# Attention and two expert blocks on one core: other start offsets for the matmul operands, and unpadded score products for two pairs of heads

## The chip, the cores and the metric

The kernel runs on one core of one Trainium2 chip. Its engines appear in the profile as PE (TensorE, the matrix engine; PEld is its loading of weights), DVE (VectorE), ACT (ScalarE), POOL (GpSimd) and SP (SyncE, which only issues transfers here). The metric is the device time of one execution in microseconds; less is better.

## What is computed

The reference, cut to what matters:

```python
def _attn_ref(q, k, v):                      # q, k, v: (2, 12, 448, 64)
    scores = scale * np.matmul(q, k.transpose(0, 1, 3, 2))
    mask = np.triu(np.ones((seq, seq), dtype=bool), k=1)
    scores = np.where(mask, -1000000000.0, scores)
    scores = scores - np.max(scores, axis=-1, keepdims=True)
    attn = np.exp(scores)
    attn = attn / (np.sum(attn, axis=-1, keepdims=True) + 1e-09)
    return np.matmul(attn, v).astype(np.float32)

def _moe_ref(x, w_in, w_out, alpha):         # x: (896, 768), w_in: (768, 2048), w_out: (2048, 768)
    h = x @ w_in
    g = np.maximum(h, 0.0) + alpha * np.minimum(h, 0.0)
    return (g @ w_out).astype(np.float32)

def _moe2_ref(x, w_in, w_out):
    h = x @ w_in
    g = np.where(h >= 1, h, np.where(h <= -1, 0.0, (h + 1) ** 2 / 4.0))
    return (g @ w_out).astype(np.float32)
```

The causal attention of 2 batches with 12 heads gives x (896 tokens by 768), which goes through two expert blocks of two matrix products each.

## The kernel before

Everything is in float32 and laid out with the features on the partitions. There are 12 pairs of heads and two batches, so six pairs belong to each batch; a pair fills 128 partitions (two heads of 64 features), and its result is one tile of x. So x has 6 tiles for each batch, `x_t[b, m]`, and the hidden layer g has 16, `g_t[b, f]`. Such a tile is 128 partitions by 2 parts by 448 columns.

The two parts are how the kernel gets precise products. A float32 value is split into a high part that fits the reduced type `float32r` and the rest; a product of two split values is made of three matmuls: high by high, high by rest, rest by high. The function `products` (line 255) does this for the layers: for each slice of 128 input features it runs six matmuls of 448 columns, three for each batch. The weights come as 64-bit floating point numbers, which five DVE and ACT operations (`split_ops`, lines 124 to 148) turn into a float32 value and split into `w_split`, one chunk at a time into three buffers in turn. A chunk is 6 slices of 128 by 128 in layers 1 and 3 and 4 slices in layers 2 and 4; a slice is loaded as the stationary operand, and a tile of x or g streams past it.

The attention of a pair has four steps i of 112 queries each, with 112, 224, 336 and 448 keys (`W`). In `scores`, the step i = 0 is a plain float32 matmul on the loaded data (line 351), and the others are split products (line 357), of which step 1 is padded from 224 to 256 columns. The two heads of a pair lie in different halves of the array's rows, and their matmuls run side by side. `split_qk` (lines 337 and 338) splits q and k of the next pair: ACT makes the high part, POOL the rest; of q, the first 112 columns, which only step 0 uses, are not split. Then follow the exponential (`expo`, ACT), the scaling with the inverse sum (`norm`, DVE and POOL), the transposes (`transp`, PE line 394), the products with v (`attnv`, PE line 413) and the splitting of the result into a tile of x (`evac`).

The order of all work is written out by hand: a loop over t = 0, 1, 2, ... runs, in each turn, the scores of step t, the exponential of step t - 1, the transposes of step t - 3 and the v products seven to nine steps later, and each engine takes its instructions in the order in which the code issues them. Pairs 3 and 4 are the turns t = 12 to 19. At the end of this loop the first products of layer 1 are mixed in (`early_tiles`). Then `run_layer` runs the four layers one after the other; in each turn PE runs the products of one output tile, while DVE, ACT and POOL split the chunk of weights that comes three turns later and work on the output tile of the turn before (the activation and its split in layers 1 and 3, `split_g`; the split of x, or the output, in layers 2 and 4). The last output tile of layer 4 is worked one batch after the other.

All tiles are whole rows of their buffers: x and g tiles of 3584 bytes a partition with their second part at byte 1792, split weights of 6144 bytes with their second part at byte 3072.

Of the kernel before, what the change touches and what calls it, by code (L numbers as in the profile page):

```python
# [9 lines left out]
F32R = mybir.dt.float32r  # L10
# [12 lines left out]
def attention_moe_moe_kernel(ctx: ExitStack, tc: tile.TileContext, qk, v, w1, w2, w3, w4, alpha, out):  # L23
# [8 lines left out]
    nc = tc.nc  # L32
    NP, _, _, S = qk.shape
    NB = 2
    CP, NQ, _, D = v.shape[1:]
# [4 lines left out]
    NF, _, KD, _ = w1.shape  # L40
    NM, NC2, _, KC, _ = w2.shape
# [3 lines left out]

    NSQ = 1
    NWARM = 9

    const = ctx.enter_context(tc.tile_pool(name="const", bufs=1))
    xpool = ctx.enter_context(tc.tile_pool(name="x", bufs=1))  # L50
    wp = ctx.enter_context(tc.tile_pool(name="wp", bufs=2))

    x_t, g_t = {}, {}

    def f32(t):
        return t.bitcast(F32)
# [6 lines left out]
    def warm_up():  # L63

        z = const.tile([128, 512], F32R, tag="zero", name="zero")
        nc.vector.memset(f32(z), 0.0)
        for _ in range(NWARM):
            ps = ps_o.tile([128, 512], F32, tag="o", name="warm_ps")
# [12 lines left out]
    class Weights:  # L81
# [29 lines left out]
        def split_ops(self):  # L111

            if self.n_split == len(self.chunks):
                return []
            n_split = self.n_split
            self.n_split += 1
            (raw, n), w = self.raw.pop(n_split), self.w.pop(n_split)
            words = raw[:, :2 * n].rearrange("p (n two) -> p n two", two=2)
            lo, hi = words[:, :, 0], words[:, :, 1]
            s = self.split[n_split] = wp.tile([128, 2, KD * 128], F32R, tag="w_split", name="w_split", bufs=3)  # L120

            def clamp():

                nc.vector.tensor_scalar(  # L124
                    out=f32(w), in0=f32(w), scalar1=HI_MIN, scalar2=HI_MAX, op0=ALU.max, op1=ALU.min
                )

            def low_bits():

                nc.vector.tensor_scalar(  # L130
                    out=w, in0=w, scalar1=5, scalar2=2, op0=ALU.logical_shift_left, op1=ALU.logical_shift_right
                )

            def high_bits():

                nc.vector.scalar_tensor_tensor(  # L136
                    out=w, in0=hi, scalar=0xC0000000, in1=w, op0=ALU.bitwise_and, op1=ALU.bitwise_or
                )

            def last_bits():  # L140

                nc.vector.scalar_tensor_tensor(  # L142
                    out=w, in0=lo, scalar=29, in1=w, op0=ALU.logical_shift_right, op1=ALU.bitwise_or
                )
                nc.scalar.copy(s[:, 0, :n], f32(w))  # L145

            def rest():
                nc.vector.tensor_sub(s[:, 1, :n], f32(w), f32(s[:, 0, :n]))  # L148

            return [clamp, low_bits, high_bits, last_bits, rest]  # L150

        def prime(self):
# [13 lines left out]
            return self.split.pop(self.n_used - 1)  # L166


    def split_g(g, b, f):
        t = g_t[b, f] = gpool.tile([128, 2, S], F32R, tag=f"g{b}_{f}", name=f"g{b}_{f}", bufs=1)  # L170
        nc.scalar.copy(t[:, 0, :], g)  # L171
        nc.gpsimd.tensor_sub(t[:, 1, :], g, f32(t[:, 0, :]))  # L172

    def act_prelu(ps, f, b):
        t = ep.tile([128, S], F32, tag="act_t", name="act_t")
        g = ep.tile([128, S], F32, tag="act_g", name="act_g")

        def negative():
            nc.vector.tensor_scalar(
                out=t, in0=ps[:, :S], scalar1=0.0, scalar2=alpha_sb[:, f:f + 1], op0=ALU.min, op1=ALU.mult  # L180
            )

        def total():
            nc.vector.scalar_tensor_tensor(out=g, in0=ps[:, :S], scalar=0.0, in1=t, op0=ALU.max, op1=ALU.add)  # L184
            split_g(g, b, f)

        return [negative, total]

    def act_quad(ps, f, b):

        t = ep.tile([128, S], F32, tag="act_t", name="act_t")
        g = ep.tile([128, S], F32, tag="act_g", name="act_g")

        def square():
            nc.vector.tensor_scalar(out=t, in0=ps[:, :S], scalar1=-1.0, scalar2=1.0, op0=ALU.max, op1=ALU.min)  # L195
            nc.scalar.activation(out=t, in_=t, func=AF.Square, bias=half[:, 0:1], scale=0.5)  # L196

        def total():
            nc.vector.tensor_tensor(out=g, in0=ps[:, :S], in1=t, op=ALU.max)
            split_g(g, b, f)  # L200

        return [square, total]

    def evac_x(ps, m, b):
        t = x_t[b, m] = xpool.tile([128, 2, S], F32R, tag=f"x{b}_{m}", name=f"x{b}_{m}", bufs=1)

        def high():
            nc.scalar.copy(t[:, 0, :], ps[:, :S])

        def low():  # L210
            nc.vector.tensor_sub(t[:, 1, :], ps[:, :S], f32(t[:, 0, :]))  # L211

        return [high, low]
# [36 lines left out]
    def products(ps, ws, src, k, kk, first, last):  # L250

        for part in range(2):
            for b in ps:
                for xp in range(2 - part):
                    nc.tensor.matmul(  # L255
                        ps[b][:, :S],
                        lhsT=ws[:, part, k * 128:(k + 1) * 128],
                        rhs=src[b, kk][:, xp, :],
                        start=first and part == 0 and xp == 0,
                        stop=last and part == 1,  # L260
                    )

    def early_tiles(batches):

        for f, bs in enumerate(batches):
            ws = wts.next()
            ps = {b: new_tile() for b in bs}
            early[f] = ws, ps
            for k in range(KD - 1):
                products(ps, ws, x_t, k, k, k == 0, False)  # L270
                yield

    def run_layer(layer, late):
# [3 lines left out]
        else:  # L277
            mt, nch, kc, src = NM, NC2, KC, g_t
        evac = {1: act_prelu, 2: evac_x, 3: act_quad, 4: evac_out}[layer]
        for m in range(mt):  # L280
            ps = {}
# [25 lines left out]
    class Attention:  # L307
# [23 lines left out]
        def split_qk(self, p, a, high=nc.scalar.copy, low=nc.gpsimd):  # L331
            t = self.raw[p]
            if a == 0:
                self.spl[p] = self.ap.tile([2 * D, 2, 2, S], F32R, tag="qk_spl", name="qk_spl", bufs=2)
            s = self.spl[p]
            n0 = NSQ * CP if a == 0 else 0
            high(s[:, a, 0, n0:], t[:, a, n0:])
            low.tensor_sub(s[:, a, 1, n0:], t[:, a, n0:], f32(s[:, a, 0, n0:]))

        def scores(self, p, i):  # L340
            if i == 0:
                self.pexp[p] = self.ap.tile([CP, 2, TRI], F32, tag="pexp", name="pexp", bufs=3)
                self.st[p] = self.ap.tile([CP, NQ, 3, 2], F32, tag="stat", name="stat", bufs=4)
            s, t = self.spl[p], self.raw[p]
            w = W[i]
            n = max(w, 256)
            ps = [self.ps_s.tile([128, 512], F32, tag="s", name="s_ps")[:CP] for _ in range(2)]
            if i < NSQ:
                for j in range(2):
                    r = slice(j * D, (j + 1) * D)  # L350
                    nc.tensor.matmul(  # L351
                        ps[j][:, :w], lhsT=t[r, 0, i * CP:(i + 1) * CP], rhs=t[r, 1, :w], start=True, stop=True
                    )
            for x, (a, b) in enumerate(self.PARTS if i >= NSQ else ()):
                for j in range(2):
                    r = slice(j * D, (j + 1) * D)
                    nc.tensor.matmul(  # L357
                        ps[j][:, :n], lhsT=s[r, 0, a, i * CP:(i + 1) * CP], rhs=s[r, 1, b, :n],
                        start=x == 0, stop=x == 2,
                    )  # L360

            for j in range(2):
                nc.vector.tensor_tensor_reduce(  # L363
                    out=self.pexp[p][:, j, OFF[i]:OFF[i] + w], in0=ps[j][:, :w], in1=mask[:, S - w:],
                    scale=-SCALE, scalar=3.0e38, op0=ALU.add, op1=ALU.min,
                    accum_out=self.st[p][:, i, 0, j:j + 1],
                )
# [50 lines left out]
        def evac(self, p):  # L418
            b, m = divmod(p, NP // NB)
            interleave(evac_x(self.o.pop(p), m, b), [])  # L420

    with tc.manual_schedule():
# [6 lines left out]
        with ExitStack() as pa:  # L429
# [21 lines left out]
            for t in range(NT + LX - 2):  # L451
                p, r = divmod(t, NQ)
# [31 lines left out]
        gpool = ctx.enter_context(tc.tile_pool(name="g", bufs=1))  # L484
# [51 lines left out]
```

## Time and profile before

| | |
|---|---|
| Runs of the kernel, us | 584.26, 586.44, 595.68; median 586.44 |
| Span of the profiled execution, first to last instruction, us | 591.80 |
| Busy time PE, DVE, ACT, POOL, us | 583.1, 442.3, 255.6, 161.6 |
| Granted TensorE clock, mean | 0.999 of full speed |

The runs are without the profiler; the profiled execution is one more, of which only the span is recorded, and its span is the time that its rows add up to. Matmuls are pipelined and the profile models their ends, so that a matmul's own duration (370 ns) is longer than the distance to the next one, and a busy PE isn't PE at its peak: the distance from start to start is what counts.

### The profile page before, as it was taken

How to read it: one execution, taken by the hardware profiler on the slowest of the kernel's cores; microseconds unless marked ns; L12 is line 12 of the kernel's file. 1: busy time of each engine (PE TensorE's matmuls, PEld its weight loads, DVE VectorE, ACT ScalarE, POOL GpSimd, SP SyncE). 2: the span in 40 equal slices, each digit the busy share in tenths (PEclk: the TensorE clock that was granted, in tenths of full speed). 3: DMA queues.
4: the chain of work that ended last, by engine and by line, in shares of the span. 5: the costliest groups of instructions: out<-in, count | busy, mean ns of one | idle time of the engine just before them, and what ended most of it. 6: DMA issues, size and time to landing. Idle time of an engine off the chain costs nothing.

```text
span 591.8 us, 8421 instructions
## 1 busy us (share of the span) xinstructions
PE 583.1 (99%) x3009; PEld 491.8 (83%) x3009; DVE 442.3 (75%) x894; ACT 255.6 (43%) x543; POOL 161.6 (27%) x190
## 2 busy tenths in 40 slices
PE   8999999999999999999999999999999999999997
PEld 3655555789999999999999999999999999999995
DVE  4899998488898898766657668888888867555740
ACT  3889888223333333333223325555555422222220
POOL 3777787223333343000000002333334300000000
PEclk9999999999999999999999999999999999999999
DMA  6533301113333222343324333333322244444420
GB/s 187 201 95 88 131 24 55 54 54 107 108 112 108 109 94 76 107 138 87 99 105 129 120 107 117 108 103 107 107 104 82 67 133 137 136 116 133 138 66 31
DMA packets 18569, 61.88 MB, mean 105 GB/s; under 512 B 2208, under 2 KB 5536, under 8 KB 18528
## 3 DMA queue, kind: packets, MB, share of 16 engines
q1 hardware_dynamic: 16656, 59.75, 32.3%
q10 hardware_dynamic: 1872, 1.61, 0.8%
q8 instruction: 23, 0.38, 0.2%
q14 instruction: 18, 0.15, 0.1%
HBM read 58.60 MB, written 2.75 MB: 104 GB/s over the span
## 4 chain that ended last, share of the span: by engine, by line
PE 95%; DVE 3%; ACT 1%; issue 0%; ACTq 0%; DVEq 0%
PE ps L255 81%; PE o_ps L413 5%; PE t_ps L394 4%; PE s_ps L357 4%; PE warm_ps L69 1%; DVE pexp L363 1%; PE s_ps L351 1%; DVE stat L380 0%; DVE pt L405 0%; DVE w_f L142 0%; DVE x L211 0%; ACT w_split L145 0%; ACT pexp L373 0%; DVE stat L381 0%; DVE pt L402 0%
## 5 line engine op out<-in xcount | busy, mean ns | idle before, releaser
L255 PE MATMUL ps<-x,w_split 128*128 128x448 f32 x1152 | 240.2, 369 | 0.2 <-DVE x L211 0.2
L255 PE MATMUL ps<-g,w_split 128*128 128x448 f32 x1152 | 238.6, 368 | 0.9 <-DVE o_sb L221 0.9
L255 PEld LDWEIGHTS ps<-x,w_split 128*128 128x128 f32 x1152 | 215.7, 188 | 24.4 <-issue 1.7
L255 PEld LDWEIGHTS ps<-g,w_split 128*128 128x128 f32 x1152 | 216.2, 188 | 23.0 <-DVE o_sb L221 1.3
L172 POOL TENSOR_TENSOR g<-act_g,g 128x448 fp32r<-128x448 f32 x64 | 85.6, 1337 | 281.4 <-ACT g L171 281.3
L145 ACT CAST w_split<-w_f 128x512 fp32r<-128x512 f32 (+1 forms) x80 | 56.6, 707 | 130.9 <-DVE w_f L142 90.9
L148 DVE TENSOR_TENSOR w_split<-w_f,w_split 128x512 fp32r<-128x512 f32 (+1 forms) x80 | 66.0, 825 | 53.6 <-ACT w_split L145 53.3
L171 ACT CAST g<-act_g 128x448 fp32r<-128x448 f32 x64 | 36.1, 564 | 79.2 <-DVE act_g L184 69.2
L136 DVE SCALAR_TENSOR_TENSOR w_f<-w_raw,w_f 128x512 uint32<-128x512 uint32 (+1 forms) x80 | 63.4, 793 | 1.4
L142 DVE SCALAR_TENSOR_TENSOR w_f<-w_raw,w_f 128x512 uint32<-128x512 uint32 (+1 forms) x80 | 63.4, 793 | 1.4
L124 DVE TENSOR_SCALAR w_f<-w_f 128x512 f32<-128x512 f32 (+1 forms) x80 | 58.1, 727 | 8.1 <-ACT w_f L108 7.9
L108 ACT ACTIVATE w_f<-w_raw 128x512 f32<-128x512 f32 (+1 forms) x80 | 61.3, 766 | 0.1
L384 POOL TENSOR_SCALAR pexp<-pexp,stat 112x112 f32<-112x112 f32 (+3 forms) x96 | 52.9, 564 | 24.4 <-DVE stat L381 19.3
L373 ACT ACTIVATE pexp<-pexp,stat 112x112 f32<-112x112 f32 (+3 forms) x96 | 49.9, 523 | 4.4 <-DVE stat L363 3.9
L363 DVE CUSTOM_DVE_ANT_0 pexp<-s_ps,mask 112x112 f32<-112x112 f32 (+3 forms) x96 | 39.1, 445 | 7.8 <-PE s_ps L351 4.6
L130 DVE TENSOR_SCALAR w_f<-w_f 128x512 uint32<-128x512 uint32 (+1 forms) x80 | 38.0, 475 | 1.4
L196 ACT ACTIVATE act_t<-act_t,half 128x448 f32<-128x448 f32 x32 | 21.5, 671 | 39.5 <-DVE act_t L195 39.5
L413 PE MATMUL o_ps<-pt,v_raw 112*64 112x448 f32 (+3 forms) x192 | 36.8, 418 | 0.0
L394 PE MATMUL t_ps<-ident,pexp 112*112 112x112 f32 x240 | 34.5, 276 | 0.0
L394 PEld LDWEIGHTS t_ps<-ident,pexp 112*112 112x112 f32 x240 | 23.9, 138 | 10.5 <-issue 5.3
L357 PE MATMUL s_ps<-qk_spl 64*112 64x256 f32 (+2 forms) x216 | 30.3, 374 | 2.2 <-DVE stat L363 2.2
L221 DVE COPY o_sb<-ps 128x224 f32<-128x224 f32 x12 | 4.7, 392 | 32.3 <-ACT o_sb L221 32.3
(38 smaller groups left out, 286.0 us busy)
## 6 DMA issues: line engine op xcount, KB each, us to landing
w_raw<-w SPq DMA_DIRECT2D x32, 768.0 KB, 4.3
w_raw<-w SPq DMA_DIRECT2D x48, 512.0 KB, 3.6
qk_raw<-qk SPq DMA_DIRECT2D x11, 448.0 KB, 3.7
v_raw<-v SPq DMA_DIRECT2D x12, 224.0 KB, 3.2
out<-o_sb SPq DMA_DIRECT2D x12, 112.0 KB, 1.7
out<-o_sb ACTq DMA_DIRECT2D x12, 112.0 KB, 1.7
qk_raw<-qk ACTq DMA_DIRECT2D x1, 224.0 KB, 3.5
qk_raw<-qk SPq DMA_DIRECT2D x1, 224.0 KB, 3.3
```

The lines of the kernel that those rows point to most:

```text
L108: nc.scalar.activation(out=f32(w), in_=f32(hi), func=AF.Abs)
L124: nc.vector.tensor_scalar(out=f32(w), in0=f32(w), scalar1=HI_MIN, scalar2=HI_MAX, op0=ALU.max, op1=ALU.min)
L136: nc.vector.scalar_tensor_tensor(out=w, in0=hi, scalar=0xC0000000, in1=w, op0=ALU.bitwise_and, op1=ALU.bitwise_or)
L142: nc.vector.scalar_tensor_tensor(out=w, in0=lo, scalar=29, in1=w, op0=ALU.logical_shift_right, op1=ALU.bitwise_or)
L145: nc.scalar.copy(s[:, 0, :n], f32(w))
L148: nc.vector.tensor_sub(s[:, 1, :n], f32(w), f32(s[:, 0, :n]))
L172: nc.gpsimd.tensor_sub(t[:, 1, :], g, f32(t[:, 0, :]))
L255: nc.tensor.matmul(ps[b][:, :S], lhsT=ws[:, part, k * 128:(k + 1) * 128], rhs=src[b, kk][:, xp, :], start=first and part == 0 and xp == 0, ...
L357: nc.tensor.matmul(ps[j][:, :n], lhsT=s[r, 0, a, i * CP:(i + 1) * CP], rhs=s[r, 1, b, :n], start=x == 0, stop=x == 2,)
L384: nc.gpsimd.tensor_scalar(out=e, in0=e, scalar1=st[:, 2, j:j + 1], scalar2=1.0, op0=ALU.mult, op1=ALU.mult)
L394: nc.tensor.transpose(ps[:, j, c, :], self.pexp[p][:, j, o:o + CP], ident)
L413: nc.tensor.matmul(ps[j * D:(j + 1) * D, c * CP:S], lhsT=vraw[:, c, j, :], rhs=pt[:, j, c, c * CP:S], start=c == 0, stop=c == NQ - 1,)
```

## The change

Two parts. First, the tiles of x and g become 24 words longer, and a tile's content starts at an offset that depends on its number (0, 8, 24, 4, 2 or 16 words of 4 bytes, taken in turn by m for x and f for g); the buffers of the split weights become 48 words longer, and their two parts start at offsets that depend on the chunk's number. Second, for the pairs 3 and 4 (`BARE`) step 0 of the scores runs as three split products of 112 columns instead of one plain float32 product, step 1 runs on 224 columns without the padding to 256, and so the whole of q is split for these pairs.

```diff
+    BARE = (3, 4)
+    PLACE = (0, 8, 24, 4, 2, 16)
+    WPLACE = ((0, 0), (8, 4), (24, 2))
...
-            s = self.split[n_split] = wp.tile([128, 2, KD * 128], F32R, tag="w_split", name="w_split", bufs=3)
+            t = wp.tile([128, 2 * (KD * 128 + max(PLACE))], F32R, tag="w_split", name="w_split", bufs=3)
+            s = self.split[n_split] = [
+                t[:, o + part * (KD * 128 + max(PLACE)):][:, :KD * 128]
+                for part, o in enumerate(WPLACE[n_split % len(WPLACE)])
+            ]
...
-                nc.scalar.copy(s[:, 0, :n], f32(w))
+                nc.scalar.copy(s[0][:, :n], f32(w))
...
-                nc.vector.tensor_sub(s[:, 1, :n], f32(w), f32(s[:, 0, :n]))
+                nc.vector.tensor_sub(s[1][:, :n], f32(w), f32(s[0][:, :n]))
...
+    def placed(pool, name, i):
+        o = PLACE[i % len(PLACE)]
+        t = pool.tile([128, 2 * S + max(PLACE)], F32R, tag=name, name=name, bufs=1)
+        return t[:, o:o + 2 * S].rearrange("p (x s) -> p x s", x=2)
+
     def split_g(g, b, f):
-        t = g_t[b, f] = gpool.tile([128, 2, S], F32R, tag=f"g{b}_{f}", name=f"g{b}_{f}", bufs=1)
+        t = g_t[b, f] = placed(gpool, f"g{b}_{f}", f)
...
     def evac_x(ps, m, b):
-        t = x_t[b, m] = xpool.tile([128, 2, S], F32R, tag=f"x{b}_{m}", name=f"x{b}_{m}", bufs=1)
+        t = x_t[b, m] = placed(xpool, f"x{b}_{m}", m)
...
-                        lhsT=ws[:, part, k * 128:(k + 1) * 128],
+                        lhsT=ws[part][:, k * 128:(k + 1) * 128],
...
-            n0 = NSQ * CP if a == 0 else 0
+            n0 = NSQ * CP if a == 0 and p not in BARE else 0
...
-            n = max(w, 256)
+            n = w if p in BARE else max(w, 256)
...
-            if i < NSQ:
+            plain = i < NSQ and p not in BARE
+            if plain:
...
-            for x, (a, b) in enumerate(self.PARTS if i >= NSQ else ()):
+            for x, (a, b) in enumerate(() if plain else self.PARTS):
```

## Rows read from the trace of the kernel before

**Rows 1.** The chain of waits: shares of the span by engine, then by line.

```profile
PE 95%; DVE 3%; ACT 1%; issue 0%; ACTq 0%; DVEq 0%
PE ps L255 81%; PE o_ps L413 5%; PE t_ps L394 4%; PE s_ps L357 4%; PE warm_ps L69 1%; DVE pexp L363 1%; PE s_ps L351 1%; DVE stat L380 0%; DVE pt L405 0%; DVE w_f L142 0%; DVE x L211 0%; ACT w_split L145 0%; ACT pexp L373 0%; DVE stat L381 0%; DVE pt L402 0%
```

**Rows 2.** Busy time by stretch: pairs 3 and 4, then the four layers.

```profile
core 0: us, PE busy (x) PEld busy (x) DVE busy (x) ACT busy (x) POOL busy (x), PEclk, DMA share, GB/s
30.90:46.20 15.30, 15.30 (x117) 9.00 (x116) 14.06 (x57) 13.37 (x45) 11.70 (x20) 1.00 0.30 92
...
121.00:238.00 117.00, 117.00 (x568) 106.27 (x567) 105.07 (x148) 41.33 (x64) 42.71 (x32) 1.00 0.29 97
240.00:358.00 118.00, 118.00 (x572) 107.19 (x571) 76.79 (x131) 35.73 (x59) 0.00 (x0) 1.00 0.38 118
360.00:477.00 117.00, 117.00 (x568) 106.28 (x567) 101.23 (x142) 61.61 (x96) 42.85 (x32) 1.00 0.31 97
479.00:584.00 105.00, 105.00 (x510) 95.38 (x509) 58.72 (x108) 26.80 (x49) 0.00 (x0) 1.00 0.38 114
```

**Rows 3.** Groups by line: the layers' products (busy us, mean ns, idle before).

```profile
L255 PE MATMUL ps<-x,w_split 128*128 128x448 f32 x1152 | 240.2, 369 | 0.2 <-DVE x L211 0.2
L255 PE MATMUL ps<-g,w_split 128*128 128x448 f32 x1152 | 238.6, 368 | 0.9 <-DVE o_sb L221 0.9
```

**Rows 4.** Timeline of PE in four windows: start, us, what, count; line 255.

```profile
104.90 2.74 PE L255 MATMUL ps<-x,w_split 128*128 128x448 f32 x12
...
108.86 2.70 PE L255 MATMUL ps<-x,w_split 128*128 128x448 f32 x12
...
112.10 2.07 PE L255 MATMUL ps<-x,w_split 128*128 128x448 f32 x9
...
115.00 1.50 PE L255 MATMUL ps<-x,w_split 128*128 128x448 f32 x6
...
117.15 1.50 PE L255 MATMUL ps<-x,w_split 128*128 128x448 f32 x6
...
119.30 1.18 PE L255 MATMUL ps<-x,w_split 128*128 128x448 f32 x3
...
239.81 105.56 PE L255 MATMUL ps<-g,w_split 128*128 128x448 f32 x510
...
559.73 24.96 PE L255 MATMUL ps<-g,w_split 128*128 128x448 f32 x120
...
585.59 0.67 PE L255 MATMUL ps<-g,w_split 128*128 128x448 f32 x2 [0.90 <-DVE o_sb L221]
...
585.59 2.70 PE L255 MATMUL ps<-g,w_split 128*128 128x448 f32 x12 [0.90 <-DVE o_sb L221]
```

**Rows 5.** Timeline of PE in pair 4; x4 and x6 of one start come from two windows.

```profile
38.55 0.45 PE L351 MATMUL s_ps<-qk_raw 64*112 64x112 f32 x4
38.94 0.59 PE L394 MATMUL t_ps<-ident,pexp 112*112 112x112 f32 x4
...
40.18 0.49 PE L357 MATMUL s_ps<-qk_spl 64*112 64x256 f32 x4
...
40.18 0.61 PE L357 MATMUL s_ps<-qk_spl 64*112 64x256 f32 x6
40.72 0.79 PE L394 MATMUL t_ps<-ident,pexp 112*112 112x112 f32 x6
...
42.80 0.98 PE L394 MATMUL t_ps<-ident,pexp 112*112 112x112 f32 x8
...
43.71 0.66 PE L357 MATMUL s_ps<-qk_spl 64*112 64x448 f32 x4
...
43.71 0.86 PE L357 MATMUL s_ps<-qk_spl 64*112 64x448 f32 x6
```

**Rows 6.** Weight loads of the plain score step: in the timeline, and over all (min/median/max, ns).

```profile
38.55 0.27 PEld L351 LDWEIGHTS s_ps<-qk_raw 64*112 64x112 f32 x4 [0.70 <-issue]
...
L351 PEld LDWEIGHTS s_ps<-qk_raw x48: 169/172/308, 9.0 to 96.2; 64*112 64x112 f32 x48
```

**Rows 7.** Groups by line and form: the splitting of q (336) and k (448).

```profile
L338 POOL TENSOR_TENSOR qk_spl<-qk_raw,qk_spl 128x448 fp32r<-128x448 f32 x11 | 12.6, 1148 | 0.0
...
L338 POOL TENSOR_TENSOR qk_spl<-qk_raw,qk_spl 128x336 fp32r<-128x336 f32 x11 | 9.9, 898 | 6.2 <-ACT qk_spl L337 6.2
...
L337 ACT CAST qk_spl<-qk_raw 128x448 fp32r<-128x448 f32 x11 | 6.2, 566 | 0.0
...
L337 ACT CAST qk_spl<-qk_raw 128x336 fp32r<-128x336 f32 x11 | 5.0, 458 | 5.2 <-DMA qk_raw<-qk 5.2
```

**Rows 8.** Timeline of POOL ahead of the pair that begins at 38.55 us.

```profile
33.75 0.90 POOL L338 TENSOR_TENSOR qk_spl<-qk_raw,qk_spl 128x336 fp32r<-128x336 f32 x1
35.04 0.69 POOL L384 TENSOR_SCALAR pexp<-pexp,stat 112x112 f32<-112x112 f32 x2 [0.40 <-DVE stat L381]
35.70 1.15 POOL L338 TENSOR_TENSOR qk_spl<-qk_raw,qk_spl 128x448 fp32r<-128x448 f32 x1
```

## The prediction

> **What bounds the kernel now.** I read the chain of waits first, then the stretches, then single runs of matmuls. The chain gives TensorE (PE) 95% of the span, and the products of the two expert blocks, line 255, 81% alone [rows 1]. The four layers fill the windows from 121 to 584 us with PE busy all of the time; VectorE (DVE) comes next, 105.07 of 117 us in the first layer and 101.23 in the third, far less in the others [rows 2]. So between 121 and 584 us the time is the number of products times their spacing, and DVE is not late until PE's layer time shrinks by a tenth. Line 255 has 2 x 1152 products [rows 3].
>
> The spacing is the thing to see. From 239.81 us on 510 products take 105.56 us; less the last one's own 0.37 us, that is 509 gaps of 0.2067 us. The 120 products from 559.73 us give (24.96 - 0.37) / 119 = 0.2066. But the last 12, which start anew at 585.59 us, lie closer: two take 0.67 us and twelve 2.70, so ten more cost 2.03, 0.203 each [rows 3, 4]. The 12 at 108.86 us take the same 2.70 us [rows 4]. So one and the same instruction has **two spacings**, 206.7 and about 203 ns; the wider one, once taken, holds over hundreds of products. Of the 2304, 48 stand ahead of 120.66 us and 12 in the last run [rows 4]; the 2,244 between are the ground on which the offsets can win or lose.
>
> Where do these operands lie? One (tile, part) of x or g is 448 words, 1792 bytes, and a 128-column slice of a split weight 512 bytes. Both are multiples of 256. So in the kernel before the starts of all streams of x and g differ by multiples of 256 bytes, those of all weight slices likewise, and the 206.7 ns holds for every k, part, batch and buffer. That excludes an effect of displacements of 256 bytes and more. Nothing in the trace tries smaller ones, and these are what the change brings (8 to 96 bytes within a tile, and 96 more bytes of length per x or g tile).
>
> In the attention stage, 30.9 to 46.2 us (the pairs 3 and 4), PE is busy 15.30 of 15.30 us, DVE 14.06, ACT 13.37, POOL 11.70 [rows 2]: what PE gains or loses there goes to the end nearly one for one, until DVE, 1.24 us behind in two pairs, takes over.
>
> **Part 1: offsets of x, g and the split weights.** No instruction is added, removed or moved; every tile gets longer by at most 192 bytes and every write keeps its shape. The cost is 2,244 times a change of the spacing. Bounds: the wider spacing is the most that the trace shows in a run without a wait, and 203 ns the least for this shape. One hint for whether starts matter: the score products are of the same kind (split operands), and their weight slices begin at multiples of 448 bytes, so at 192, 128 and 64 bytes within 256. At 448 columns their third round costs 0.86 - 0.66 = 0.20 us, at 256 columns 0.61 - 0.49 = 0.12 [rows 5]: 0.45 and 0.47 ns per column, against 0.45 at the closer spacing of line 255 (203 / 448). Other weight starts, the same rate. It looks like a property of the stream, and the wider spacing like the way in which products settle against each other in time. I take **0**; the low end is that all products go to the closer spacing, 2,244 x (206.7 - 203) ns = **-8.3 us**. The high end is a loss of the same size, the only step between spacings that the trace has: six start offsets, of which one is 0, so at 5/6 of the products 2,244 x 5/6 x 3.7 ns = **+6.9 us**.
>
> The Trainium skill (TensorE: Matmul & The Clock Gate, Part 2, step 1) says that TensorE has two independent SBUF read ports, one for the streamed operand and one for the weight load, and that loading the next weights takes no bandwidth from the running matmul. By that rule the placing of x against the weights can't matter and the term is 0; that the spacing takes two values with the same operands, 206.7 and 203 ns [rows 4], shows at least that something beyond the columns enters. The skill (SBUF — State Buffer, Door 1) also states 16-byte lines with a penalty at each crossing; a start 8 bytes into a line makes 113 lines of 112, an estimate of 1/112 of 206.7 ns, 1.8 ns, at the tiles that have that offset (one x tile in six, two g tiles in sixteen: 336 products), 0.6 us. No run here shows it.
>
> The writers: ACT, DVE and POOL write the shifted tiles with the same shapes. Their cover is DVE's 12 us of slack in layer 1 and 16 us in layer 3, and 41 to 46 us in the others [rows 2]; gone only if DVE got 11% slower. Cost 0.
>
> **Part 2: the first two score steps of pairs 3 and 4.** In step 0 a head's plain float32 product (two instructions of 112 columns) becomes three split products of 112 columns. Both heads run side by side, so it is two rounds becoming three. In step 1 three rounds shrink from 256 to 224 columns. Nothing in the trace streams split operands under 256 columns, so I bound it.
> Low end: the stream goes on as it does above 256 columns, and a round lasts as long as the longer of its stream and its weight load. Step 1: a round falls from 0.12 us by 32 x 0.45 ns, three rounds -0.04 us. Step 0: the four weight loads take 0.27 us, of which one's own 0.17 is the tail, so a round of loading is 0.10 us [rows 6]; three such rounds stand for two of about 0.09 to 0.10 (the eight transposes of 112 columns take 0.39 us more than the first four, 0.10 each [rows 5]), the last with 0.05 us less to stream: +0.05 us. Sum 0.01 us a pair.
> High end: under 256 columns a split product costs as much as a plain one. A plain product of 112 columns takes two instructions of some 0.095 us (by the 0.09 to 0.10 above), 0.19; step 0: two more of them, +0.38 us. Step 1: 224 columns cost 0.38 instead of 0.12, three times, +0.78. Sum 1.16 us a pair, **+2.3 us** for both.
> I take the low end, **+0.0**, by the nearest row, the 256-column rounds: the same instruction on the same operands, 32 columns away. Below nothing there is little room: the whole of step 1 is 40.72 - 40.18 = 0.54 us [rows 5].
>
> The q half is now split over 448 instead of 336 columns for these pairs: ACT 0.57 for 0.46 us, POOL 1.15 for 0.90 [rows 7]. On POOL the split of q ends 0.40 us before the next scaling can start, which waits for DVE [rows 8], so 0.25 us are covered; without that cover the k half and the next transposes behind it on POOL would come 0.25 us later. ACT has 1.93 us idle in the two pairs [rows 2]. Step 0 now waits for the split of both halves instead of the raw load; the k half of the pair that begins at 38.55 us is done at 35.70 + 1.15 = 36.85 us, 1.7 us ahead [rows 5, 8]. Cost 0.
>
> **The sum.** 0 + 0.0 + 0 on the profiled execution: its span of 591.80 us stays at about 591.8. The three runs are 584.26, 586.44 and 595.68, so the profiled execution lies between the second and the third. That spread, 11.4 us, is not much more than the 8.3 us between the two spacings over 2,244 products: the runs may differ in how much of each holds the wider spacing. So the run with the median may already lie close, and I carry the difference of 0 to the median: **586.5 us**.
>
> **The rivals.**
> 1. *The shifted starts break the wide spacing.* For it: the wide spacing is one exact value held by 500 products, as two streams in step would give; each k brings another offset and would knock them out of step. Against: the score products above. Gain up to 8.3 us on a run that is wide throughout, less on one that is not: 578 to 584 us, 579 as one number. Chance 0.20.
> 2. *The excess over the clock is a conflict of addresses, and the offsets remove it.* PE's granted clock is 1.00, the 2.4 GHz level [rows 2]; one cycle per column is 186.7 ns for 448 columns, and the plain 112-column instructions come within 2 or 3 ns of their 93.3 (two cycles a column). Without conflicts the spacing would be near 189, 17 ns less, 2,244 x 17 ns = 38 us: 548 us. DVE would still not bind (layer 1: 117 x 189/206.7 = 107 us, DVE 105.07). Against: the score products show the same excess at other weight starts, and it grows with the columns, as the 0.12 and 0.20 us show. Chance 0.06. The isolated matmul of the TensorE page (Back-to-back issue gap) is N/2.4 + 2.5 ns, 189.2 at 448 columns, the same result; the trace has 206.7 and 203.
> 3. *Slower: a start inside a fetched piece of the memory costs each shifted stream one more piece.* It strikes at 5/6 of the products and is never hidden, since PE has no other work. At 3.7 ns it gives 6.9 us, with the high end of part 2 9.2 us: 593 to 596 us. It decides against rival 1 as soon as it exceeds 3.7 ns at each shifted product, and passes 2% (11.7 us) from 6.3 ns. Against: nothing in the trace shows a start that costs. Chance 0.16, of which 0.07 beyond 2%.
> The case that is left is the forecast itself, in which part 1 does not do what offsets could be meant to do, since the products settle against each other whatever their starts: 586.5 us, chance 0.58.
>
> **How the numbers follow.** Two per cent, 11.7 us, is about what a measurement of this kernel can tell from no change. Faster by more (under 574.7): rival 2 and a tail of rival 1, 0.09. Slower by more (over 598.2): 0.07 of rival 3 and 0.01 for part 2 on top of a wide-spaced median, 0.08. Within: 0.83. The range reaches over rival 1 and over rival 3 up to 2%, and takes in a median that lies with the slower of the runs shown: 577 to 597 us.
>
> **What would show it.** If part 1 is right, long runs of line 255 keep 0.2067 us a product, in all four layers. If rival 1 holds, the spacing is mixed, near 0.203; if rival 2, near 0.19; if rival 3, it exceeds 0.207 at the shifted tiles. Part 2 is seen in the score groups of pairs 3 and 4: six products of 112 columns in about 0.5 us and six of 224 in about 0.57 by the low end, 0.83 and 1.4 by the high end, beside 0.45 and 0.61 for pairs that are not changed. The forecast goes wrong if starts within 256 bytes matter to the stream, and little else can move it far.

## The result, and the profile after

The changed kernel took 588.95, 590.07, 593.88 and 593.94 us, median 591.98; the kernel before, with one run more, 584.26, 584.91, 586.44 and 595.68, median 585.67. The ratio is 1.011, 95% interval 1.008 to 1.015: a small loss, inside the forecast range (577 to 597 us) and within 2%, but not the difference of 0 that was forecast.

These times don't scatter around one value. In all timings together the kernel before shows two levels, one around 585 us and one around 594 (a few executions near 599), with little between; 41 of its 82 executions lay above 590 us. In the three series below the granted clock was 0.999 to 1.000 at either level, so it isn't the clock. The share of the upper level was 3 of 24 in the first of them, 21 of 25 in the second and 16 of 29 in the third, and each ran on another chip. A ratio to this kernel therefore depends on how many executions of either level it meets, and below each kernel is set beside the level that it is compared with.

The profiled execution of the changed kernel has a span of 587.2 us, the one of the kernel before had 591.80: in these two executions the changed kernel is the shorter one. The chain by line is still that of [rows 1]: the layers' products, now line 271, 80%.

```profile
PE 95%; DVE 3%; ACT 1%; issue 0%; ACTq 0%; DVEq 0%
PE ps L271 80%; PE o_ps L430 5%; PE t_ps L411 4%; PE s_ps L374 4%; PE warm_ps L76 1%; DVE pexp L380 1%; PE s_ps L368 1%; DVE stat L397 0%; DVE pt L422 0%; DVE w_f L153 0%; DVE x L227 0%; ACT w_split L156 0%; ACT pexp L390 0%; DVE stat L398 0%; DVE pt L419 0%
```

The stretches of [rows 2], here layers 1 and 2 of the kernel after: PE has no gap in layer 2, DVE still has its slack, and more products fit into the same 118 us (580 instead of 572).

```profile
core 0: us, PE busy (x) PEld busy (x) DVE busy (x) ACT busy (x) POOL busy (x), PEclk, DMA share, GB/s
...
121.00:238.00 117.00, 116.80 (x572) 107.17 (x571) 105.72 (x149) 41.64 (x65) 42.11 (x32) 1.00 0.29 97
240.00:358.00 118.00, 118.00 (x580) 108.69 (x579) 78.41 (x134) 36.47 (x61) 0.00 (x0) 1.00 0.38 118
```

The timeline of PE merges products that follow each other without a gap, and a whole layer (96 turns of six) can stand in one row. That makes it the best view for the spacing: (duration - 0.37) / 575. First the kernel before, a window that was not shown with [rows 4], then the kernel after.

```profile
229.88 119.20 PE L255 MATMUL ps<-g,w_split 128*128 128x448 f32 x576
348.93 119.20 PE L255 MATMUL ps<-x,w_split 128*128 128x448 f32 x576
```

```profile
229.75 117.68 PE L271 MATMUL ps<-g,w_split 128*128 128x448 f32 x576
347.26 117.67 PE L271 MATMUL ps<-x,w_split 128*128 128x448 f32 x576
```

That is 206.7 ns before and **204.0 ns** after. From single starts to the next, the trace of before holds 206 or 207 ns through layers 2 and 3; the one after holds everything from 195 to 215 ns, with a mean of 204.0 (the timeline's rows give means; these single distances are taken from the starts of the matmuls in the traces, here and below).

The score steps of pairs 3 and 4, to be read beside [rows 5]: six products of 112 columns in 0.50 us, six of 224 in 0.58 and 0.56, where four plain ones took 0.45 and six of 256 columns 0.61.

```profile
31.93 0.50 PE L374 MATMUL s_ps<-qk_spl 64*112 64x112 f32 x6
...
33.61 0.58 PE L374 MATMUL s_ps<-qk_spl 64*112 64x224 f32 x6
...
38.25 1.65 PE L430 MATMUL o_ps<-pt,v_raw 112*64 112x448 f32 x4
39.83 0.50 PE L374 MATMUL s_ps<-qk_spl 64*112 64x112 f32 x6
...
41.50 0.56 PE L374 MATMUL s_ps<-qk_spl 64*112 64x224 f32 x6
```

### The profile page after: what moved, and what is told of

It reads as the page before. It is cut to its first block, busy times and chain, and to the rows that moved or that the text cites. A ratio compares the mean times of both kernels' runs of the same rounds, so it can differ in the third digit from the quotient of the medians.

```text
span 587.2 us, 8431 instructions
## 1 busy us (share of the span) xinstructions
PE 578.4 (99%) x3013; PEld 493.1 (84%) x3013; DVE 441.5 (75%) x894; ACT 256.3 (44%) x543; POOL 161.0 (27%) x190
## 4 chain that ended last, share of the span: by engine, by line
PE 95%; DVE 3%; ACT 1%; issue 0%; ACTq 0%; DVEq 0%
PE ps L271 80%; PE o_ps L430 5%; PE t_ps L411 4%; PE s_ps L374 4%; PE warm_ps L76 1%; DVE pexp L380 1%; PE s_ps L368 1%; DVE stat L397 0%; DVE pt L422 0%; DVE w_f L153 0%; DVE x L227 0%; ACT w_split L156 0%; ACT pexp L390 0%; DVE stat L398 0%; DVE pt L419 0%
## 5 line engine op out<-in xcount | busy, mean ns | idle before, releaser
L271 PE MATMUL ps<-x,w_split 128*128 128x448 f32 x1152 | 237.3, 367 | 0.2 <-DVE x L227 0.2
L271 PE MATMUL ps<-g,w_split 128*128 128x448 f32 x1152 | 235.6, 366 | 0.9 <-DVE o_sb L237 0.9
L188 POOL TENSOR_TENSOR g<-act_g,g 128x448 fp32r<-128x448 f32 x64 | 84.3, 1317 | 278.1 <-ACT g L187 278.1
L374 PE MATMUL s_ps<-qk_spl 64*112 64x448 f32 (+4 forms) x228 | 31.8, 374 | 2.2 <-DVE stat L380 2.2
L374 PEld LDWEIGHTS s_ps<-qk_spl 64*112 64x112 f32 x228 | 18.4, 190 | 14.8 <-DVE stat L380 6.1
```

Of the source, the lines that this page charges most:

```text
L271: nc.tensor.matmul(ps[b][:, :S], lhsT=ws[part][:, k * 128:(k + 1) * 128], rhs=src[b, kk][:, xp, :], start=first and part == 0 and xp == 0, ...
L374: nc.tensor.matmul(ps[j][:, :n], lhsT=s[r, 0, a, i * CP:(i + 1) * CP], rhs=s[r, 1, b, :n], start=x == 0, stop=x == 2,)
```

## The experiments

**First question: which part?** Four kernels with one part each. `offsets_only` is the changed kernel with `BARE = ()`; `bare_only` the kernel before with the unpadded score steps; the other two shift only x and g or only the weights:

```diff
 # offsets_only
-    BARE = (3, 4)
+    BARE = ()
 # xg_offsets_only: as offsets_only, and the weights as before
-            t = wp.tile([128, 2 * (KD * 128 + max(PLACE))], F32R, tag="w_split", name="w_split", bufs=3)
+            t = wp.tile([128, 2 * KD * 128], F32R, tag="w_split", name="w_split", bufs=3)
...
 # w_offsets_only: as offsets_only, and x and g as before
-        t = pool.tile([128, 2 * S + max(PLACE)], F32R, tag=name, name=name, bufs=1)
-        return t[:, o:o + 2 * S].rearrange("p (x s) -> p x s", x=2)
+        t = pool.tile([128, 2 * S], F32R, tag=name, name=name, bufs=1)
+        return t.rearrange("p (x s) -> p x s", x=2)
```

> All shifted starts (x, g and split weights), all pairs of heads scored as before. Theory A (the shifted starts set another spacing of the layers' products): this alone gives the whole 1.1%, 590 to 594 us, and in its profile the spacing of line 271's kind of product is mixed between 195 and 215 ns with a mean of 204 to 206. Theory B (the loss sits in the score steps of pairs 3 and 4, which also shift the moment at which the layers begin): this comes out within 0.3% of the kernel before.

> Only the unpadded score steps of pairs 3 and 4, all tiles at their old places. Theory A: within 0.2% of the kernel before, the two steps of a pair together within 0.1 us of before, and the layers' spacing one of the two values of before (206.7 or 203 ns). Theory B: 1.1% slower.

> Shifted starts for the streamed tiles x and g alone. If only the streamed operand's start matters, this has the whole of the 1.1% and the mixed spacing, and its products with the tile that starts 8 bytes off are the slowest, 205 to 207 ns. If only the start relative to the weights matters, it has some of it. If only the weights' start matters: within 0.2% and an unmixed spacing.

> Shifted starts for the split weights alone. The reverse of the run before: within 0.2% and an unmixed spacing if only the streamed operand matters, the 1.1% if only the weights do.

Measured on one chip, with the kernel before at a median of 585.11 us (24 executions, 3 of them above 590): `bare_only` 585.57 us, ratio 1.0005 (0.9997 to 1.0014); `offsets_only` 588.49, 1.0066 (1.004 to 1.0091); `xg_offsets_only` 588.21, 1.0051 (1.0039 to 1.0062); `w_offsets_only` 587.50, 1.0043 (1.0019 to 1.0067). So theory B falls and the offsets are the cause, by either operand alone, each with a part of it (0.5% and 0.4%) and not with the whole or nothing. Theory A had the spacing right (204.0 ns in the trace of `offsets_only`); its time, 590 to 594 us, was too large, for against the lower level of the kernel before the whole of the offsets is 0.6%, not 1.1%.

The rows of whole layers say why. The timeline of `bare_only`, whose tiles lie as in the kernel before:

```profile
228.57 116.90 PE L256 MATMUL ps<-g,w_split 128*128 128x448 f32 x576
345.30 116.90 PE L256 MATMUL ps<-x,w_split 128*128 128x448 f32 x576
```

(116.90 - 0.37) / 575 = 202.7 ns, through whole layers, in an execution of 585.4 us. The kernel before has the same tiles and held 206.7 ns in its profiled one. Over 2,244 products the two differ by 9.0 us, which is the distance between its two levels. So the tiles of the kernel before allow **two patterns that repeat**: one of 206.7 ns, and one in which the distances run through 198 to 208 ns with a mean of 202.67. The traces with shifted starts hold neither, but a wider mixture. It comes with the starts: `offsets_only`, another execution with other work in the score steps, repeats it to 0.01 us a layer.

```profile
229.27 117.68 PE L271 MATMUL ps<-g,w_split 128*128 128x448 f32 x576
346.79 117.67 PE L271 MATMUL ps<-x,w_split 128*128 128x448 f32 x576
```

The shifted kernels have a rarer upper level too: 593.54 us in one of seven executions of `offsets_only`, 592.84 in one of twelve of `w_offsets_only`, 593.9 in two of the four on record. None of these executions was traced, so their spacing is not known.

**Second question: which start costs?** Taken from the starts of the matmuls in the trace of the changed kernel, the mean distance by the streamed tile's offset:

```
offset in the tile, bytes     0      32     96     16     8      64
mean distance, ns           204.1  203.5  203.9  204.0  205.4  203.2
```

Byte 8 stands out. It does so in `xg_offsets_only` too (205.7 ns, as expected of it), but there byte 64, the closest in this table, comes near it with 205.2, and byte 0 has 202.9. `offsets_only` repeats the table to 0.1 ns and differs from `xg_offsets_only` in the weights alone, so an offset of the stream has no fixed price of its own. Four kernels give all x and g tiles one and the same offset (`START` is 0, 2, 4 or 8 words, that is byte 0, 8, 16 or 32), with tiles 64 bytes longer than before, weights and scores as before:

```diff
-        o = PLACE[i % len(PLACE)]
-        t = pool.tile([128, 2 * S + max(PLACE)], F32R, tag=name, name=name, bufs=1)
+        o = START
+        t = pool.tile([128, 2 * S + 16], F32R, tag=name, name=name, bufs=1)
```

> Control: every x and g tile is 64 bytes longer, every content starts at byte 0 of its tile, split weights as before, no unpadded scores. If the starts within a 64-byte stretch decide, the spacing is that of bare_only's profile, 202.67 ns, and the time within 0.1% of the kernel before. If the longer tiles themselves (the distance between tiles) cost, it is 203.4 to 204 ns and 0.3 to 0.5% slower.

> As start_0, but every x and g tile starts at byte 8. If a start 8 bytes off is what costs (205.4 to 205.7 ns at these tiles in the mixed kernels), all products go to about 205.5 ns: 2244 x 2.8 ns = +6.4 us, 1.1%. If what costs is that starts differ from product to product, a uniform start of 8 bytes keeps 202.67 ns.

> As start_0, but every x and g tile starts at byte 16. If the cost comes from starts inside a 16-byte line, 202.67 ns and no change. If it comes from the start relative to the weights' start, or from a line of 32 or 64 bytes, 203 to 205 ns, 0.2 to 0.9% slower.

> As start_0, but every x and g tile starts at byte 32. 202.67 ns if lines of 32 bytes or less decide; 203 to 205 ns if 64 bytes or the start relative to the weights do.

Beside these four kernels, 21 of the 25 executions of the kernel before lay above 590 us (median 594.15), so I set them beside its lower level, here four executions at 584.7 to 585.5 us. Medians: `start_0` 586.12 us, `start_8_bytes` 592.24 (all ten at 591.7 to 593.0), `start_16_bytes` 585.27 (four executions), `start_32_bytes` 588.12 (two of ten at 592.8). Layers 2 and 3 of the timelines of byte 0, 8, 16 and 32, in this order:

```profile
228.22 117.28 PE L270 MATMUL ps<-g,w_split 128*128 128x448 f32 x576
345.34 117.05 PE L270 MATMUL ps<-x,w_split 128*128 128x448 f32 x576
```

```profile
230.49 118.58 PE L270 MATMUL ps<-g,w_split 128*128 128x448 f32 x576
348.92 118.77 PE L270 MATMUL ps<-x,w_split 128*128 128x448 f32 x576
```

```profile
228.53 116.64 PE L270 MATMUL ps<-g,w_split 128*128 128x448 f32 x576
345.01 117.07 PE L270 MATMUL ps<-x,w_split 128*128 128x448 f32 x576
```

```profile
229.50 117.60 PE L270 MATMUL ps<-g,w_split 128*128 128x448 f32 x576
346.94 117.28 PE L270 MATMUL ps<-x,w_split 128*128 128x448 f32 x576
```

Means over all layers: 203.1, 205.7, 202.6 and, at byte 32, 203.6 ns. Three things follow. The distance between tiles alone, 64 bytes more with the start at 0, is enough to lose both patterns of before; that was the second branch of `start_0`, at a smaller size (203.1 where it said 203.4 to 204). Byte 8 costs, as expected. And byte 32 is worse than byte 16, so lines of 16 or 32 bytes do not sort the cases. The Trainium skill (SBUF — State Buffer, Door 1) states 16-byte lines, by which bytes 0, 16 and 32 should be alike, and they are not (203.1, 202.6, 203.6). Nor is it order against disorder: in layers 2 and 4 the distances of these kernels repeat too, every 12 products at byte 0 and every 36 at the other three, and in layers 1 and 3 of the changed kernel every 108, the products of three chunks of weights.

**Third question: the streamed operand's own start, or its start beside the weights'?** Two kernels leave x and g as in the kernel before and move only the weights, in buffers 512 bytes longer, so that all distances stay multiples of 512 bytes (`WSTART` is 2 words, byte 8, in one kernel and 124 words, byte 496, in the other):

```diff
+    WSTART = 2
...
-            s = self.split[n_split] = wp.tile([128, 2, KD * 128], F32R, tag="w_split", name="w_split", bufs=3)
+            t = wp.tile([128, 2 * KD * 128 + 128], F32R, tag="w_split", name="w_split", bufs=3)
+            s = self.split[n_split] = t[:, WSTART:WSTART + 2 * KD * 128].rearrange("p (x n) -> p x n", x=2)
```

With them ran the changed kernel and the kernel of byte 16 once more.

> Tiles of x and g as in the kernel before; each buffer of the split weights is 512 bytes longer and its content starts at byte 8. If a start 8 bytes off costs the streamed operand itself (205.7 ns with all x and g at byte 8), this has 202.7 ns or, in step, 206.7. If it is the start relative to the weights that costs, this is near 205.7 ns, 592 us, as well.

> As weights_8_bytes with the weights at byte 496, so that every stream of x and g lies 16 bytes past the weights' start within 512, the distances of all tiles being multiples of 512 bytes. If the relative start decides and 16 bytes is good (198 ns at such pairs in layers 2 and 4 of the start_16 kernel), the spacing falls to 198 to 201 ns, 576 to 582 us. If history and distance between tiles decide, one of the old spacings, 202.7 or 206.7 ns, 585 or 594 us.

> The changed kernel once more, for the size of the difference. Theory A2: the changed starts put the spacing at a fixed mixture of 204.0 ns, and the distance to the kernel before depends on which of its two spacings (202.7 or 206.7 ns) that kernel takes: +3 us beside executions of 585 us, -5 us beside executions of 594 us. Rival: the changed kernel has an extra cost of its own beyond the spacing and is 1.1% slower again beside 585 us (592 us).

> Every x and g tile 64 bytes longer with its content at byte 16, for whether it keeps away from the wide spacing. Theory A2: tiles whose distance is not a multiple of 512 bytes never fall into step, so all executions lie at 585 to 586 us, none at 593 or more. Rival (the two values belong to the execution, not to the addresses): an execution in eight or more lies 8 us higher here too.

Beside these four, 16 of the 29 executions of the kernel before lay above 590 us (median 593.59), the 13 others at 584.6 to 586.0. `weights_8_bytes` took **579.49 us**, all six executions within 579.2 to 580.0; the ratio on record, to the kernel before with executions of both levels in it, is 0.986 (0.981 to 0.992), and beside the median of the 13 lower ones alone (585.52) it is 0.990. Both branches of its expectation were wrong. Its layers:

```profile
227.08 115.36 PE L257 MATMUL ps<-g,w_split 128*128 128x448 f32 x576
342.28 115.36 PE L257 MATMUL ps<-x,w_split 128*128 128x448 f32 x576
```

(115.36 - 0.37) / 575 = 200.0 ns, and single distances are 200 ns almost without exception (2,257 of 2,303): a third pattern, closer than both of the kernel before. It is not the only one of this layout: the 12 products from 105.69 us and the last 12 of the same trace run through 201 to 207 ns instead. `weights_496_bytes` shows the same 115.36 us a layer in its profiled execution, of 579.6 us; but only 6 of its 12 executions lie at 579 to 581 us, five at 586 to 588 and one at 592 (median 583.39, ratio 0.991, 0.985 to 0.997). The first branch of its expectation, 576 to 582 us, thus held in half of the executions. Its trace, too, has another series, with a mean of 203.1 ns in the last 12 products; over 2,244 products that would be 7 us more, an estimate from these few rows. It fits the five, of which none was traced.

So a move of the weights alone, with x and g as they were, changes the spacing from 202.7 or 206.7 to 200.0 ns: the stream's own start does not decide, but **the starts of stream and weights together**, with the distances between tiles. That only their difference counts is not shown, for no kernel moves x, g and the weights by the same amount; nor was the longer weight buffer tried with its content at byte 0.

The changed kernel again: 589.22 us median of 12 executions, 11 of them at 588.1 to 590.9, one at 594.0; ratio to the kernel before beside it 1.002 (0.997 to 1.007). Theory A2 holds in the main: against the lower level (585.5 us) it loses 3.7 us, against the upper one (594) it wins 5. The rival's 592 us falls; two of the first four executions on record were of the rare upper sort. `start_16_bytes` again: 585.09 us, 11 of 12 at 584.5 to 585.6, one at 590.5. It does not fall to 593 as the kernel before does, but "none higher" was too much.

## Why the prediction was right where it was, and where it failed

**What bounds the kernel** held: PE has all of the layers, DVE stayed behind it even where the spacing fell to 200.0 ns (99.99 of 110 us from 125 us on, in layer 1 of `weights_8_bytes`; 99.42 in the changed kernel), and the differences of several microseconds between these kernels are the spacing times the number of products. `weights_8_bytes` against the closer pattern of before: 2,244 x (202.7 - 200.0) = 6.1 us, measured 585.52 - 579.49 = 6.0. Beside that the layers don't begin at the same time: their long run starts at 120.55 to 122.01 us in the traces, and at 121.31 and 121.96 in the two of the changed kernel alone.

**Two spacings** held too, and more fully than the text said: the closer one, seen then only after two restarts [rows 4], runs through whole executions. The guess that the runs of the kernel before differ in how much of them is wide is borne out in so far as the same layout of tiles was seen at 206.7 ns in its own trace and at 202.7 in that of `bare_only`, and the 9.0 us between them is the distance between its two levels. What makes an execution take the one or the other is open; the share changed from series to series, and with it the chip. Within one execution a restart can switch it: in the trace of before the 12 products from 104.90 us hold 206 or 207 ns, the 12 from 108.86 repeat 199, 207, 202, 203 and 202, and the long run from 120.66 us is wide again.

**Part 1 taken as 0 was the step that failed.** The text took the spacing for a property of the stream, to which starts do nothing. They do: 204.0 ns beside 202.7, 2,244 x 1.35 ns = +3.0 us, between the chosen 0 and the high end of +6.9. The high end itself was met by the kernel with all x and g at byte 8 (592.24 us, 6.9 above the lower level; 205.7 - 202.7 = 3.0 ns a product). The hint on which the 0 rested, the same rate of score products at several weight starts, was too short to see this: three rounds cannot settle into a pattern, and a difference of 1.4 ns is a hundredth of their 0.12 us, below what rows in hundredths of a microsecond show. That 591.98 us lies inside the range all the same is owed to the range, which was drawn to hold a loss by rival 3 and a slower median, and not to the sum.

The rule of the Trainium skill that was set beside it (TensorE: Matmul & The Clock Gate, Part 2, step 1), two independent read ports and so no loss by the next weight load, gives the same 0, and the trace speaks against that reading: moving the weights by 8 bytes, in buffers 512 bytes longer, with x and g as they were took 2.7 ns off the closer spacing and 6.7 off the wider one.

**The rivals.** Rival 1, shifted starts break the wide spacing, is right as a mechanism in the traces, and wrong in its sign beside executions of the lower level: the starts break the closer pattern as well. On an execution of the wide kind the changed kernel is indeed ahead, 587.2 us of span against 591.80. Rival 3, a loss at shifted streams, named the side, and at byte 8 nearly the size (3.7 ns where 3.0 was measured), but its price for any shifted start is refuted by byte 16 and by the moved weights. Rival 2, down to 189 ns, was not reached; 200.0 ns is the least seen.

**Part 2** held in its main point: unpadded split products are not charged as plain ones. Step 0 costs 0.05 us more and step 1 0.03 to 0.05 less, as the low end said; the high end (0.83 and 1.4 us) is out. The cover of the longer split of q, counted as complete, was not. In the turn before each of the two pairs the product with v waits longer for DVE's copy of the transposed probabilities. The weight loads of PE ahead of pair 4, in the kernel before and after:

```profile
37.19 0.19 PEld L413 LDWEIGHTS o_ps<-pt,v_raw 112*64 112x64 f32 x2
37.66 0.19 PEld L413 LDWEIGHTS o_ps<-pt,v_raw 112*64 112x64 f32 x2 [0.28 <-DVE pt L405]
```

```profile
38.25 0.19 PEld L430 LDWEIGHTS o_ps<-pt,v_raw 112*64 112x64 f32 x2
38.93 0.19 PEld L430 LDWEIGHTS o_ps<-pt,v_raw 112*64 112x64 f32 x2 [0.49 <-DVE pt L422]
```

In `bare_only` the four v products of these turns take 1.71 and 1.66 us; with the short split they take 1.48 and 1.44 in the kernel before and 1.36 and 1.43 in `offsets_only`. So it is some 0.2 us a pair, 0.35 at most. The 0.40 us on POOL that the prediction read as slack [rows 8] are none. The scaling behind the split needs DVE's inverse sums, and the first DVE instruction for these (line 380 before, 382 in `bare_only`, 397 in `offsets_only`), which takes 0.17 us where POOL is idle, here lasts until POOL's split of q is done. First `bare_only`, then `offsets_only`, ahead of pair 4:

```profile
34.37 1.14 POOL L339 TENSOR_TENSOR qk_spl<-qk_raw,qk_spl 128x448 fp32r<-128x448 f32 x1
...
34.42 1.11 DVE L382 TENSOR_SCALAR stat<-stat 112x2 f32<-112x2 f32 x1
```

```profile
34.66 0.90 POOL L354 TENSOR_TENSOR qk_spl<-qk_raw,qk_spl 128x336 fp32r<-128x336 f32 x1
...
34.70 0.88 DVE L397 TENSOR_SCALAR stat<-stat 112x2 f32<-112x2 f32 x1
```

The two end within 0.03 us of each other ahead of both pairs in the traces of these two kernels, of before and of after, and POOL's wait before the scaling is 0.40 us with the long split as with the short one. That DVE's copy comes late for this reason is argued from the order of its instructions. The whole of part 2 is 0.05% (1.0005, -0.03 to 0.14%), 0.3 us: inside its bounds of 0.0 to 2.3, and too little to matter.

**The sum** of 586.5 us thus missed +3 us from the starts and some 0.3 us from part 2, and the rest of the distance to the 591.98 on record is that two of four executions lay at 594; in twelve later ones the median was 589.2. What spacing the executions at 594 held stays open.

## What to carry to other kernels

Where a kernel is one long stream of matmuls, read the distance from start to start in rows that merge a whole stretch: a difference of 1% there is the whole game, and it can come from nothing but where the operands lie. Before offsets are spread over many values, try one offset for the weights alone: such a layout can settle into a good pattern (200.0 ns, 579.5 us, 1.0% ahead of the lower level of the kernel before and 1.7% ahead of the changed kernel), where the mixed ones of this case ran at means of 203.8 to 204.0. It need not do so in every execution: with the weights at byte 496 half of them did, with byte 8 all six. And when a kernel has two levels of time, compare level with level before explaining a ratio of medians.

## What was not expected of the hardware

A matmul of 448 columns of split operands, with the granted clock at 1.00 (the 2.4 GHz level), never came to the 186.7 ns of one column a cycle. The kernel before and the two with moved weights settled at 200.0, 202.7 (as a mean of a repeating series) or 206.7 ns, which are 480, 486.4 and 496 cycles; the other layouts gave means of 202.6 to 205.7. Why these, and by what exact rule of addresses, is open: sorting single distances by the starts of the streams and of the weights within 512 bytes did not give one table that fits all kernels.

POOL's subtraction that makes the low part of g was faster into tiles whose content starts at byte 8. Groups by line and form, for `start_0` and `start_8_bytes`:

```profile
L187 POOL TENSOR_TENSOR g<-act_g,g 128x448 fp32r<-128x448 f32 x64 | 85.8, 1341 | 275.0 <-ACT g L186 275.0
```

```profile
L187 POOL TENSOR_TENSOR g<-act_g,g 128x448 fp32r<-128x448 f32 x64 | 73.1, 1142 | 292.1 <-ACT g L186 292.1
```

1341 against 1142 ns for the same work, on an engine that had time to spare here. The changed kernel separates it from the rest of the layout: there the eight of these instructions whose tiles start at byte 8 take 1156 ns on average and those at each of the other five offsets 1330 to 1346; `start_16_bytes` and `start_32_bytes` have 1338 and 1337. Why byte 8 is the faster one is open.

An instruction of DVE on 112x2 values took 0.17 us where POOL was idle and up to 1.15 us beside POOL's split of q, ending with it, as the rows of part 2 show. Why it is held so long is open.
